# Slot attention and GELU FFN on one core: the first two batches take turns by 4, 4 and 8 chunks, with whole-chunk decoding in a new pinned order

## The chip, the cores and the metric

One core of a Trainium2 chip runs the whole program. The metric is the device time of one execution in microseconds (us), taken as the median of several runs. Lower is better.

## What is computed

Inputs are q, k, v (8 batches x 8 heads x 576 x 64), phi (8 x 8 x 576 x 32), and the weights w_in (512 x 2048) and w_out (2048 x 512).

```python
a = exp(phi - phi.max(axis=2)); a /= a.sum(axis=2) + 1e-9        # over the 576 positions
k_m = einsum('bhsm,bhsd->bhmd', a, k)                            # 32 slots per head
v_m = einsum('bhsm,bhsd->bhmd', a, v)
s = (q @ k_m.T) / sqrt(64)
p = exp(s - s.max(-1)); p /= p.sum(-1) + 1e-9
x = (p @ v_m).transpose(0, 2, 1, 3).reshape(4608, 512)           # heads side by side
h = x @ w_in
out = (0.5 * h * (1 + erf(h / sqrt(2)))) @ w_out
```

The result is float32. The weights arrive as float64 and are handed over as pairs of 32-bit words.

## The kernel before

**Algebra.** x is never formed. For each batch, v_m is multiplied into w_in first, which gives U (256 slots x 2048), and the hidden layer is p times U. Every float32 factor of the large products is split into a high part (fp32r) and a low part, and each product is three matmuls: high by high, high by low, low by high.

**Steps.** The 2048 columns of d_ff are 16 chunks f of 128. A step is one chunk of one batch: `hidden` (L671) runs 12 matmuls of 288 columns (two halves `hf` of the 576 rows) into the PSUM tag h; `gelu` (L685) on ScalarE writes gf; `gelu_hi` (L693) copies gf to gh, and `gelu_lo` (L696) on VectorE subtracts gh from gf to make gl; `project` (L714) runs 12 matmuls of 512 columns (L710) into four PSUM accumulators, acc0 to acc3. The products of a step are issued behind the hidden matmuls of the next one. The last 64 rows of each batch are collected in `tails` and projected for two batches at a time.

**Turns.** The batches come one after the other, 16 steps each, but the first two alternate: chunks 0 to 7 of batch 0, 0 to 7 of batch 1, 8 to 15 of batch 0, 8 to 15 of batch 1 (L657). One accumulator set serves one turn. At the end of a turn `evict` (L736) empties it: at the end of the first turn of a batch by a copy to an SBUF tile `part` (accumulators 0 and 2 by VectorE, 1 and 3 by ScalarE), at the end of the last turn by adding `part` and the accumulator into the output tile (L748, on VectorE).

**Decoding.** While batches 0 and 1 run, each chunk of the weights is turned from float64 words to float32, 512 columns of w_in and 512 of w_out: `dec_b` on ScalarE (L202, L203), `dec_c` on VectorE (L207, L208), `dec_s` on VectorE (L214), `dec_d` on GpSimd (L224, one add for each half), and for w_out the split into wo_hi on ScalarE (`dec_e`) and wo_lo on VectorE (`dec_f`, L230). In `dec_b`, `dec_c` and `dec_s` a second argument picks one half (128x512); without it both are done at once (128x1024).

**U and the scores.** `u_p` (L628) makes pu, a product of v_m with decoded w_in, for 1, 2 or 4 chunks; `u_h` and `u_l` (L634, L639) split it into U, on ScalarE and VectorE. `UPS` (L804) says how many chunks one such piece takes for batch 0; batch 1 always takes 4. The scores of batch 1 (psc, then `sT`, `max`, `sub`, `exp`, `sum`, `inv`, `mul`, `pT`, `ph`, `pl`) go on beside the first steps. pu, the scores psc and the slot sums pk share one PSUM buffer pair, so each of them waits until the one ahead of it has been read out.

**Order.** `START` (L22) is a list of pieces that pins the order of every engine's instructions from the program's begin into step 20 or so: names with batch, half or chunk, as `dB.3.0` for the first half of `dec_b` of chunk 3, `p.0.2` for the products of batch 0, chunk 2, and `gh.0.3:a` for a piece placed on ScalarE. Behind it, `put` gives each piece a due time in half steps, and the loop at L882 issues what is due. `prepare` (L807) puts there what a later batch needs for its softmax over phi: loads, maxima, the exponentials `aexp` with their sums, and `anat` (`a_nat`, L357), which adds the negated maxima to phi in its natural layout and takes the exponential again, for 512 rows and then for the last 64. Between `gelu` and an exponential ScalarE loads another function table.

## Time and profile before

| | us |
|---|---|
| median of 3 runs (lowest, highest) | 735.03 (734.57, 737.3) |
| profiled execution, own time | 736.67 |
| its span in the profile | 734.9 |

| engine | busy us | share of the span |
|---|---|---|
| TensorE (PE) | 712.2 | 97% |
| VectorE (DVE) | 395.5 | 54% |
| ScalarE (ACT) | 349.5 | 48% |
| GpSimd (POOL) | 47.9 | 7% |

The mean granted TensorE clock was 0.997 of its full level. Start times below count from the span's start. Between two instructions of one engine the starts are closer together than the busy times, since neighbours overlap a little: where the text speaks of what an instruction costs its engine, it is the distance from its start to the next one's.

### The profile page before, as it was taken

The numbers are of one execution on the slowest core, as the hardware profiler recorded it, in microseconds if no ns is written. First come the engines' busy times: TensorE is split into PE (matmuls) and PEld (weight loads), VectorE is DVE, ScalarE is ACT, GpSimd is POOL, SyncE is SP. The second block draws the span as 40 slices with busy tenths as digits, with TensorE's granted clock in tenths as the row PEclk, the third lists the DMA queues.
The fourth block names the chain that finished last, engine by engine and source line by source line (L and its number), as shares of the span: only waits on it lengthen the run. The fifth ranks groups of instructions, "written<-read, shape, count | busy, mean of one in ns | idle before, by whom it ended". The sixth has DMA issues, their size and how long they took to land.

```text
span 734.9 us, 12195 instructions
## 1 busy us (share of the span) xinstructions
PE 712.2 (97%) x4958; PEld 580.6 (79%) x4958; DVE 395.5 (54%) x686; ACT 349.5 (48%) x715; POOL 47.9 (7%) x45
## 2 busy tenths in 40 slices
...
GB/s 292 349 207 120 50 220 100 131 1 185 137 105 90 106 135 95 1 237 62 33 1 58 193 63 33 1 204 15 47 1 58 47 33 0 1 58 1 1 1 71
DMA packets 42584, 65.15 MB, mean 89 GB/s; under 512 B 2848, under 2 KB 24992, under 8 KB 42528
## 3 DMA queue, kind: packets, MB, share of 16 engines
...
q14 instruction: 17, 0.14, 0.1%
...
## 4 chain that ended last, share of the span: by engine, by line
PE 87%; DVE 4%; ACT 3%; issue 3%; DMA 2%; SPq 0%; POOL 0%; ACTq 0%; DVEq 0%; POOLq 0%
PE acc L710 45%; PE h L678 26%; PE tacc L710 6%; PE pu L439 4%; DMA kv<-kv 2%; PE psc L381 1%; PE psc L439 1%; PE psc L456 1%; DVE raw L208 1%; PE pk L381 1%; DVE gl L697 1%; DVE y L207 1%; ACT L688 0%; ACT L298 0%; DVE o L748 0%
## 5 line engine op out<-in xcount | busy, mean ns | idle before, releaser
L678 PE MATMUL h<-p_hi,U 128*128 128x288 f32 x1024 | 207.2, 301 | 2.6 <-ACT tails L691 1.3
L710 PE MATMUL acc<-wo_hi,gh 128*128 128x512 f32 x512 | 202.9, 397 | 0.0
L710 PE MATMUL acc<-wo_hi,gl 128*128 128x512 f32 x512 | 201.6, 394 | 0.0
L710 PE MATMUL acc<-wo_lo,gh 128*128 128x512 f32 x512 | 201.3, 393 | 0.0
L678 PEld LDWEIGHTS h<-p_hi,U 128*128 128x128 f32 x1024 | 165.2, 190 | 24.4 <-issue 6.3
L155 DVE CAST gh<-gf 128x512 fp32r<-128x512 f32 x108 | 46.0, 426 | 209.5 <-ACT gf L690 209.3
L688 ACT ACTIVATE gf<-h 128x288 f32<-128x288 f32 x128 | 52.8, 412 | 220.2 <-issue 160.2
L710 PEld LDWEIGHTS acc<-wo_hi,gh 128*128 128x128 f32 x512 | 96.1, 188 | 33.9 <-DVE gh L155 6.7
L710 PEld LDWEIGHTS acc<-wo_hi,gl 128*128 128x128 f32 x512 | 96.1, 188 | 22.7 <-DVE gh L155 0.8
L678 PE MATMUL h<-p_lo,U 128*128 128x288 f32 x512 | 110.6, 298 | 0.4 <-DVE p_lo L534 0.4
L710 PEld LDWEIGHTS acc<-wo_lo,gh 128*128 128x128 f32 x512 | 96.1, 188 | 17.4 <-issue 0.4
L697 DVE TENSOR_TENSOR gl<-gf,gh 128x512 fp32r<-128x512 f32 x128 | 89.9, 702 | 10.2 <-ACT gh L155 2.1
L678 PEld LDWEIGHTS h<-p_lo,U 128*128 128x128 f32 x512 | 83.8, 190 | 2.0 <-DVE p_lo L534 1.0
L690 ACT ACTIVATE gf<-h 128x224 f32<-128x224 f32 x128 | 45.6, 356 | 40.5 <-PE h L678 40.3
L688 ACT ACT_TABLE_LOAD x30 | 38.5, 1283 | 19.0 <-PE h L678 17.3
L641 DVE TENSOR_TENSOR U<-pu,U 128x1024 fp32r<-128x1024 f32 (+2 forms) x39 | 40.0, 1025 | 12.6 <-ACT U L155 12.3
L155 ACT CAST U<-pu 128x1024 fp32r<-128x1024 f32 (+2 forms) x39 | 33.8, 867 | 20.2 <-PE pu L439 20.1
L439 PE MATMUL pu<-w_in_sb,kT 64*32 64x512 f32 (+2 forms) x624 | 38.0, 531 | 2.5 <-DVE U L641 2.1
L208 DVE SCALAR_TENSOR_TENSOR raw<-raw 128x512 int32<-128x512 int32 (+1 forms) x33 | 36.6, 1108 | 0.3
L691 ACT ACTIVATE tails<-h 128x64 f32<-128x64 f32 x128 | 28.3, 221 | 0.0
L224 POOL TENSOR_TENSOR w_in_sb<-y,raw 128x512 int32<-128x512 int32 x16 | 23.0, 1440 | 54.8 <-DVE y L214 51.0
L202 ACT ACTIVATE y<-raw 128x512 f32<-128x512 f32 (+1 forms) x33 | 22.9, 695 | 7.7 <-DVE wo_lo L230 3.7
...
## 6 DMA issues: line engine op xcount, KB each, us to landing
...
```

The source lines that it names most:

```text
L155: return e.copy(dst, src) if e is nc.scalar else e.tensor_copy(dst, src)
L202: nc.scalar.activation(y, high.bitcast(F32), AF.Abs, scale=2.0**16)
L208: nc.vector.scalar_tensor_tensor(low, high, -(2**31), low, op0=ALU.bitwise_and, op1=ALU.bitwise_or)
L224: nc.gpsimd.tensor_tensor(w, y, low, op=ALU.add)
L439: nc.tensor.matmul(ps[g][M * j : M * j + M], st["kT", b][rows, t, M * j : M * j + M], moving[rows, j, :], start=True, stop=True,)
L641: nc.vector.tensor_sub(u[:, :, 1], st["pu", b, f], u[:, :, 0].bitcast(F32))
L678: i = nc.tensor.matmul(h[:, :HS], u[g][w], x[:, g, :], start=(n == 0), stop=(n == 3 * G - 1))
L688: nc.scalar.activation(gf[:, :HS], h[:, :HS], AF.Gelu)
L690: nc.scalar.activation(gf[:, HS:], h[:, : MAIN - HS], AF.Gelu)
L691: nc.scalar.activation(tails()[:, f, b % 2], h[:, MAIN - HS : HS], AF.Gelu)
L697: nc.vector.tensor_tensor(g_of("gl", b, f), g_of("gf", b, f), g_of("gh", b, f).bitcast(F32), op=ALU.subtract)
L710: nc.tensor.matmul(acc, x, w[:, f, :], start=(first and n == 0), stop=(last and n == 2))
```

## The change

- The first two batches take turns by chunks 0 to 3, 4 to 7 and 8 to 15, so there are six turns where there were four. The middle turn finds a `part` there already, and `evict` adds its accumulators to it, all four on VectorE.
- `a_nat` does both additions first (the 64 rows ahead of the 512) and then both exponentials; `prepare` puts `aexp` and `anorm` beside `anat`, at `tn + 1` in place of `t + 3`.
- U of batch 0 is made for single chunks 0 to 3 and then for pairs 4 and 6 (singles 0 to 7 before).
- `START` is written anew. Chunk 0 alone is decoded in halves, the others whole, with instructions of 1024 columns; k and v of batch 0, and part of q, are loaded ahead of the first weights. Chunk 15, which before was decoded by halves in START and then once more in whole by the due times (33 `dec_b` pairs in all), is decoded once (17 pairs in all).

```diff
 START = """
-Lphi.0.0 Lphi.0.1 Lwi.0 amax.0.0 Lwo.0 amax.0.1 aexp.0.0 aexp.0.1 Lkv0.0.0 at.0.0.0
...
+Lphi.0.0 Lphi.0.1 Lkv0.0.0 amax.0.0 Lkv0.1.0 amax.0.1 aexp.0.0 aexp.0.1 Lq.0.0 at.0.0.0
+anorm.0 at.0.1.0 atc.0.0.0 at.0.0.4 Lwi.0 atc.0.1.0 at.0.1.4 atc.0.0.4 atc.0.1.4
...
     def a_nat(b):
 
         aT, pn, full = st["aT", b], st["pn", b], S // P
-        for x, r, n in ((aT[:, :full], 0, full), (aT[P - TL :, full:], P - TL, 1)):
+        xs = ((aT[P - TL :, full:], P - TL, 1), (aT[:, :full], 0, full))
+        for x, r, n in xs:
             nc.vector.tensor_tensor(
                 x, x, pn[r:].unsqueeze(1).to_broadcast([P - r, n, G, P]), op=ALU.add
             )
+        for x, _, _ in xs:
             nc.scalar.activation(x, x, AF.Exp)
...
     steps = []
-    for b, lo, hi in [(b, lo, lo + NF // 2) for lo in (0, NF // 2) for b in range(2)] + [
-        (b, 0, NF) for b in range(2, B)
-    ]:
+    turns = [(b, lo, hi) for lo, hi in ((0, 4), (4, 8), (8, NF)) for b in range(2)]
+    for b, lo, hi in turns + [(b, 0, NF) for b in range(2, B)]:
         steps += [(b, f, f == lo, f == hi - 1) for f in range(lo, hi)]
...
         a = st["acc", b, f][j]
+        if f < NF - 1 and ("part", b, j) in st:
+            nc.vector.tensor_add(st["part", b, j], a, st["part", b, j])
+            return
         if f < NF - 1:
...
-    UPS = {f: 1 for f in range(NF // 2)} | {8: 4, 12: 2, 14: 2}
+    UPS = {f: 1 for f in range(4)} | {4: 2, 6: 2, 8: 4, 12: 2, 14: 2}
...
-        put(t + 3, *(f"aexp.{b}.{g}" for g in range(G)), f"anorm.{b}", f"dg.{b}")
+        put(t + 3, f"dg.{b}")
         put(tn - 1, f"Lphin.{b}")
-        put(tn + 1, f"anat.{b}")
+
+        put(tn + 1, f"anat.{b}", *(f"aexp.{b}.{g}" for g in range(G)), f"anorm.{b}")
```

The whole program's instructions by engine, before and now: TensorE rows 2667 and 2665, VectorE 665 and 624, ScalarE 697 and 658 (function table loads 70 and 68), GpSimd 51 and 51, SyncE 170 and 169. These count rows of the engines' program, in which repeated instructions can share a row.

**Place 1: ScalarE, around the first p_hi copies** (`n_hi`: L530 before, L526 now; s_2 is the last part of batch 0's scores, U_0 the first U). Before:

```order
L487 ACTIVATE s_1_250<-s_1_250 128x512
L202 ACTIVATE y_317<-raw_256 128x512
L203 ACTIVATE raw_256<-raw_256 128x512
L155 COPY kT_204<-tn_202 128x128
L202 ACTIVATE y_317<-raw_256 128x512
L203 ACTIVATE raw_256<-raw_256 128x512
L155 CAST U_0_342<-pu_0_333 128x2x128
L487 ACTIVATE s_2_349<-s_2_349 128x256
L530 CAST p_hi_0_372<-pT_0_311 128x288
```

Now:

```order
L483 ACTIVATE s_2_355<-s_2_355 128x256
L149 COPY aT_330<-pt_4_357 64x128 x2
L149 CAST U_0_378<-pu_0_369 128x2x128
L196 ACTIVATE y_390<-raw_338 128x1024
L197 ACTIVATE raw_338<-raw_338 128x1024
L526 CAST p_hi_0_419<-pT_0_300 128x288
L526 CAST p_hi_0_419<-pT_1_302 128x288
L526 CAST p_hi_1_430<-pT_0_300 128x224
L526 CAST p_hi_1_430<-pT_1_302 128x224
L526 CAST p_hi_1_430<-pT_2_425 128x64 x2
```

The decoding of chunk 2 (raw_256 before, raw_338 now) stood ahead of the last exponential and of the U copy, in halves; now it stands whole, directly ahead of the p_hi copies.

**Place 2: VectorE, up to the gl of batch 0, chunk 3** (gl_3). Before:

```order
L697 TENSOR_TENSOR gl_2_651<-gf_2_601,gh_2_637 128x512
L641 TENSOR_TENSOR U_0_342<-pu_3_641,U_0_342 128x2x128
L207 TENSOR_SCALAR y_654<-y_654 128x512
L208 SCALAR_TENSOR_TENSOR raw_545<-raw_545 128x512
L547 STREAM_TRANSPOSE sT_0_682<-psc_0_663 128x288
L230 TENSOR_TENSOR wo_lo<-y_561,wo_hi 128x512
L547 STREAM_TRANSPOSE sT_0_682<-psc_0_663 128x288
L214 TENSOR_SCALAR y_654<-y_654 128x512
L558 TENSOR_REDUCE mx_0_713<-sT_0_682 128x18
L207 TENSOR_SCALAR y_654<-y_654 128x512
L208 SCALAR_TENSOR_TENSOR raw_545<-raw_545 128x512
L565 TENSOR_TENSOR sT_0_682<-sT_0_682,mx_0_713 128x576
```

Now:

```order
L692 TENSOR_TENSOR gl_2_693<-gf_2_622,gh_2_675 128x512
L224 TENSOR_TENSOR wo_lo<-y_545,wo_hi 128x512
L208 TENSOR_SCALAR y_651<-y_651 128x1024
L569 TENSOR_REDUCE smx_1_729<-sT_1_657 128x18
L575 TENSOR_SCALAR smx_1_729<-smx_1_729 128x18
L576 RECIPROCAL smx_1_729<-smx_1_729 128x18
L581 TENSOR_TENSOR sT_1_657<-sT_1_657,smx_1_729 128x576
L587 STREAM_TRANSPOSE pT_1_739<-sT_1_657 128x576
L637 TENSOR_TENSOR U_0_705<-pu_0_696,U_0_705 128x2x512
L605 TENSOR_TENSOR p_lo_1_748<-pT_1_739,p_hi_1_741 128x576
L692 TENSOR_TENSOR gl_3_762<-gf_3_715,gh_3_746 128x512
```

Before, the first half of batch 1's scores (sT_0) was begun here; now its second half (sT_1) is finished here and the U of batch 1's first four chunks is made, since batch 1 begins behind chunk 3.

**Place 3: VectorE at the end of the turn of batch 0's chunks 4 to 7, now** (gl_4 belongs to batch 1, chunk 4; the part tiles are batch 0's):

```order
L692 TENSOR_TENSOR gl_7_1142<-gf_7_1112,gh_7_1139 128x512
L201 TENSOR_SCALAR y_1145<-y_1145 128x1024
L202 SCALAR_TENSOR_TENSOR raw_1099<-raw_1099 128x1024
L224 TENSOR_TENSOR wo_lo<-y_1060,wo_hi 128x512
L692 TENSOR_TENSOR gl_4_1188<-gf_4_1163,gh_4_1185 128x512
L735 TENSOR_TENSOR part_0_823<-acc_4_0_1038,part_0_823 128x512
L735 TENSOR_TENSOR part_1_827<-acc_4_1_1039,part_1_827 128x512
L735 TENSOR_TENSOR part_2_825<-acc_4_2_1040,part_2_825 128x512
L735 TENSOR_TENSOR part_3_830<-acc_4_3_1041,part_3_830 128x512
```

The four additions stand directly behind a gl, in one piece; before there was no turn end at this place.

## Rows read from the trace of the kernel before

**Rows 1.** Windows: us, PE, PEld, DVE, ACT, POOL busy (count), PEclk, DMA share, GB/s.
```profile
0.00:20.00 20.00, 13.97 (x128) 11.95 (x128) 5.89 (x16) 9.21 (x19) 3.53 (x9) 1.00 0.94 294
20.00:40.00 20.00, 16.91 (x163) 13.12 (x163) 16.89 (x42) 11.85 (x27) 2.64 (x2) 1.00 1.00 334
40.00:60.00 20.00, 16.52 (x187) 11.97 (x187) 19.64 (x30) 14.00 (x32) 8.66 (x6) 0.95 0.52 179
60.00:80.00 20.00, 17.93 (x159) 13.51 (x158) 18.69 (x34) 15.85 (x31) 5.72 (x4) 0.96 0.25 83
...
59.00:61.00 2.00, 2.00 (x14) 1.98 (x9) 1.86 (x5) 0.50 (x2) 0.03 (x1) 0.50 0.37 48
```

**Rows 2.** Waits of PE: total us, times, longest.
```profile
PE pu L439 <- DVE U L641: 2.1, 2, 1.1
PE psc L439 <- DVE U L641: 1.8, 1, 1.8
```

**Rows 3.** Timeline of PE before 90 us: start, us, engine, line, operation.
```profile
66.17 0.45 PE L439 MATMUL pu<-w_in_sb,kT 64*32 64x128 f32 x16 [1.08 <-DVE U L641]
...
84.86 0.54 PE L678 MATMUL h<-p_hi,U 128*128 128x288 f32 x2 [1.12 <-ACT U L155]
...
88.05 0.40 PE L710 MATMUL acc<-wo_hi,gh 128*128 128x512 f32 x1
```

**Rows 4.** Chain of waits, one full step: start, us, what.
```profile
96.93 2.77 PE acc L710 x12
99.70 1.59 PE h L678 x12
```

**Rows 5.** Timeline of PE, a U product of four chunks.
```profile
122.64 1.09 PE L439 MATMUL pu<-w_in_sb,kT 64*32 64x512 f32 x16
```

**Rows 6.** Timeline of DVE, two stretches.
```profile
39.03 0.34 DVE L534 TENSOR_TENSOR p_lo<-pT,p_hi 128x64 fp32r<-128x64 f32 x2
...
43.15 0.69 DVE L208 SCALAR_TENSOR_TENSOR raw<-raw 128x512 int32<-128x512 int32 x1
43.77 0.67 DVE L697 TENSOR_TENSOR gl<-gf,gh 128x512 fp32r<-128x512 f32 x1
44.36 0.74 DVE L214 TENSOR_SCALAR y<-y 128x512 int32<-128x512 int32 x2
...
46.48 1.80 DVE L208 SCALAR_TENSOR_TENSOR raw<-raw 128x512 int32<-128x512 int32 x1
...
89.80 1.21 DVE L641 TENSOR_TENSOR U<-pu,U 128x1024 fp32r<-128x1024 f32 x1
90.93 0.67 DVE L697 TENSOR_TENSOR gl<-gf,gh 128x512 fp32r<-128x512 f32 x1
```

**Rows 7.** Timeline of POOL beside them.
```profile
46.24 1.49 POOL L224 TENSOR_TENSOR w_in_sb<-y,raw 128x512 int32<-128x512 int32 x1
```

**Rows 8.** Groups of DVE by form, 0 to 160 us: busy us, mean ns, idle before.
```profile
L208 DVE SCALAR_TENSOR_TENSOR raw<-raw 128x512 int32<-128x512 int32 x32 | 35.3, 1104 | 0.3
...
L208 DVE SCALAR_TENSOR_TENSOR raw<-raw 128x1024 int32<-128x1024 int32 x1 | 1.2, 1218 | 0.0
...
L207 DVE TENSOR_SCALAR y<-y 128x1024 f32<-128x1024 f32 x1 | 0.7, 682 | 0.0
```

**Rows 9.** ACT: a group by form of 0 to 160 us, and its timeline near 33.
```profile
L202 ACT ACTIVATE y<-raw 128x1024 f32<-128x1024 f32 x1 | 1.1, 1132 | 0.0
32.94 1.20 ACT L530 CAST p_hi<-pT 128x288 fp32r<-128x288 f32 x4 [0.21 <-PE pT L515]
```

**Rows 10.** Timeline of ACT, an exponential between two gelus.
```profile
152.24 1.28 ACT L298 ACT_TABLE_LOAD   x1
153.53 0.78 ACT L298 ACTIVATE phi<-phi,nm 128x576 f32<-128x576 f32 x1
```

**Rows 11.** Timeline of PE and DVE, 167 to 171 us.
```profile
167.40 0.54 PE L678 MATMUL h<-p_hi,U 128*128 128x288 f32 x2 [1.00 <-ACT tails L691]
...
170.55 1.88 DVE L748 TENSOR_TENSOR o<-acc,part 128x512 f32<-128x512 f32 x3
```

83 lines of the change are left out of this document (38 added, 45 removed).

## The prediction

> **What bounds the kernel now.** I read the windows first, then TensorE's waits, its timeline up to 100 us, the chain of waits, and last VectorE's and GpSimd's rows of the same stretch. TensorE is busy 712.2 of 734.9 us, so 22.7 us is all that a new order can win unless TensorE's own work changes. The windows show where that idle time lies: 6.0 us in the first 20, 3.1, 3.5 and 2.1 in the next three windows of 20 [rows 1]. From the product at 88.05 on, TensorE's groups follow each other at 2.77 us (12 products) and 1.59 us (12 hidden matmuls), 4.36 us a step [rows 3, 4], and the largest wait behind that is one of 1.0 us at 167 [rows 11]. So the gain, if any, is made before 88 us. There the window rows show VectorE busy for 19.64 and 18.69 of 20 us [rows 1], and TensorE's waits name it: for the U subtraction at L641, because pu and psc share one buffer pair [rows 2, 3]. From about 39 us to 91 us the kernel goes at VectorE's pace. Up to 40 us it goes at the pace of the transfers: the DMA share is 0.94 and 1.00, at 294 and 334 GB/s [rows 1].
>
> **Term 1, the start.** The change loads k, v and q of batch 0 ahead of the weights. On ScalarE the whole decoding of chunk 2 now stands directly ahead of the p_hi copies (the first place shown), so these wait for that chunk's transfer. In SyncE's new order the bytes up to the w_out rows of chunk 2 are, from the shapes, 0.59 (phi 0) + 2.36 (k, v 0) + 1.18 (q 0) + 2.10 (chunks 0, 1) + 0.59 (phi 1) + 2.10 (eight pieces of k, v 1) + 1.05 (chunk 2) = 9.97 MB. At the rates of before, 5.88 MB pass by 20 us and the other 4.1 MB need 12.2 us: 32.2, and I allow 1 us for landing: 33.2. The two ScalarE instructions of 1024 columns, 1.13 each [rows 9], end at 35.5. VectorE's L208 on the result, 1.14 (1.22 busy less the overlap of 0.08 that neighbours show) [rows 8], ends at 36.6, and the p_lo subtractions behind it (288, 224 and 64 columns, two each, about 1.6 by the width of the 512-wide rows) at 38.2. Meanwhile the p_hi copies, 1.20 for four and about 0.3 for the short pair [rows 9], have ended at 37.0 and are covered. Before, the last p_lo ended at 39.3 [rows 6]. **Gain 1.1 us.** The bounds: with landing in 0 us 2.1, with landing 2 us later nothing or a loss of 1.
>
> **Term 2, eight steps at VectorE's pace.** Take VectorE from the last p_lo to the gl of the eighth step (batch 0, chunk 7 before; batch 1, chunk 3 now). Costs are distances between starts [rows 6]: L208 of 512 columns 0.62, a gl 0.59, L214 0.335 (two in 0.67; L207 of the same width like it), U of four chunks 1.13; whole-chunk L207 and L214 0.60 (0.68 busy less the overlap) [rows 8]. By the order, what differs in the stretch is this:
> - L208: 12 halves, 7.4, become 6 whole, 6.8: 0.6 less; I count 0.4, since the overlap of a whole one is known from a single row.
> - L207 and L214: 24 halves, 8.0, become 12 whole, 7.2: 0.8 less.
> - U: two of four chunks and six single ones, 2.26 + 6 x 0.335 = 4.3, become one of four, two pairs (0.60, as any 512 wide) and three single ones, 3.3: 0.9 less.
> - Two copies to `part` at the first turn's end, 0.6 each: 1.2 more. The other two are ScalarE's.
>
> Eight gl, seven wo_lo and the two score sets of batch 1 stand on both sides. Together 0.9 us less. But VectorE does not go at these costs: all 81 instructions of the stretch make 39.5 us by them, and it took from 39.3 to the end of the gl at 90.93, 91.5 [rows 6], that is 52.2, or 1.32 times as long. The surplus is what GpSimd's adds cost it: an L208 took 0.69 where none ran and 1.80 beside the add at 46.24 [rows 6, 7], and the mean of 32 is 1.10 [rows 8]. The adds are 12 on both sides. So 0.9 x 1.32 = **1.25 us gained**: the eighth gl ends at 38.2 + 38.55 x 1.32 = 89.1, where before it was 91.5.
>
> **Term 3, TensorE's own work.** Four single U products of 0.38 (66.17 to the next start, 66.55) [rows 3] become two pairs of about 0.59, between that and the 1.02 of four chunks (1.09 busy) [rows 5]: **0.35 us less**.
>
> **What I cost at nothing.** The eight additions to `part` (8 x 0.6 = 4.8 us of VectorE) lie between 88 and 150 us, where TensorE has no waits; in the same stretch whole-chunk decoding and the second decoding of chunk 15 that is gone give some of it back. Without that cover each turn's end would cost up to what its additions reach past the 1.59 us of the next hidden matmuls: 2.4 - 1.6 = 0.8. The three additions in a row at 170.55, 1.88 us, held up no matmul [rows 11]. The regrouped exponentials save table loads on ScalarE (1.28 each [rows 10]); they can win part of the 1.0 us at 167, and I set 0.5 of it against 0.5 of new waits at the hand-over from batch 0 to batch 1, whose U and scores must now be ready four steps earlier. What is late next is the same thing as before, VectorE, four steps into each turn.
>
> **Sum.** 1.1 + 1.25 + 0.35 = 2.7 us. The profiled execution took 736.67 and would come to 734.0; the median of the runs is 735.03, 1.64 lower, and the forecast is made against it: **732.3 us**. Its own range is 729.5 to 735. A measurement of this kernel can tell about 0.5% from no change, 3.7 us: under 731.4 counts as faster, over 738.7 as slower.
>
> **Rivals.**
> - *GpSimd's adds miss VectorE.* With half as many instructions on VectorE and new neighbours, the adds may fall on instructions that they do not delay. The mean L208 lost 1.10 - 0.69 = 0.41 to them [rows 6, 8]; without this for 12 adds, 4.9 us: 732.3 - 4.9 = **727.4**. For it: the next bound, TensorE, leaves room, since eight steps at 4.36 are 34.9 of the 51 us. Against: adds and L208 belong to the same chunk chain, so they come close together again. Chance 0.25.
> - *The adds hit every time.* An add of 1.49 held up one L208 by 1.80 - 0.69 = 1.11 [rows 6, 7]. If each of the 12 met a long instruction, 12 x (1.11 - 0.41) = 8.4 more: **740.7**. Whole-chunk instructions are twice as long and so easier to meet, but the mean of before says that two in three were not met in full. Chance 0.04. The Trainium skill, page "SBUF — State Buffer", section Terms, has VectorE and GpSimd lock a shared port pair for a whole instruction, so that the loser "fully blocks". By that rule this rival is what any add would do when a VectorE instruction that needs the pair comes behind it; the trace agrees at the one place shown, where the L208 ended 0.55 us after the add at 47.73, nearly its whole length.
> - *The gain is given back at the turns' ends.* There are two more of them, at up to 0.8 us each if VectorE is still late there, and at the two middle ones VectorE has two additions of 0.6 that would have been ScalarE's copies, of which I let one reach past the hidden matmuls: 2 x 0.8 + 2 x 0.6 = 2.8 us: 735.1, say **735**. For it: VectorE stays above 90% busy in these windows. Against: the row at 170.55. Chance 0.11.
> - *Slower: the first step waits for the weights.* The p_hi copies have no way round the decoding of chunk 2 on ScalarE. If the chunk lands at 38 and not at 33.2, because the eight pieces of k and v of batch 1 and phi 1 ahead of it in the queue go slower, all eight steps begin 4.8 us later, and term 1 turns from +1.1 to -3.7. TensorE then stands nearly idle from 34 on, and its clock falls, as it did in the window 59 to 61, behind the wait for psc: 0.50 granted, that is 1.2 GHz, and a product group or hidden group of 1.59 takes near twice that [rows 1, 4]. I price it at 1.6 for such a group, and 0.8 for the turn's end that is then missed: 732.3 + 4.8 + 1.6 + 0.8 = **739.5**. It decides from a landing at about 36 on; the DMA was saturated over these 40 us, which speaks for it, and the byte count, which is a sum and no guess, against it. Chance 0.14.
>
> **How the numbers follow.** Forecast 0.46, the others 0.25, 0.04, 0.11 and 0.14. The range that should hold 8 in 10 reaches from just under the second case, 726.5, to just over the slower one, 740.0; the forecast's own is 729.5 to 735. A third of the forecast's chance lies under 731.4: faster is 0.25 + 0.15 = 0.40; no difference is 0.31 + 0.11 = 0.42; slower 0.14 + 0.04 = 0.18.
>
> **What would show it.** In the profile of the changed kernel: the last short p_lo pair ends near 38.2 (term 1; 41 or later is the slower rival, with p_hi copies released by L197 late). The gl of batch 1, chunk 3, ends near 89 (term 2), and VectorE stays above 90% busy from 40 to 90; if that gl ends by 85 the adds missed, and the mean of whole-chunk L208 is near 1.2, not 1.5 to 1.8. TensorE's waits still name L641. Behind 90 us there is no wait of TensorE over 1 us, and none released by an addition to `part`; if there are, the third rival holds. The prediction is wrong if TensorE's idle time before 90 us changes by more than 5 us either way, or if TensorE's busy time changes by more than 1.

## The result, and the profile after

The changed kernel took 740.88 us (median of 6 runs, 738.57 to 743.13), the kernel before 735.21 (6 runs beside it, 734.57 to 737.3). The ratio is 1.0073 [1.0059, 1.0086]: slower by 5.4 us, where a gain of 2.7 was forecast, and outside the range. The profiled execution took 740.40 us, 3.73 more than the one of before. All ratios below are against the kernel before, run on the same chip at the same time; start times come from one profiled execution of each kernel. In the changed kernel the products stand at L705, the hidden matmuls at L673, gl at L692, the subtraction of U at L637, and the decoding at L196 (ScalarE), L202 and L208 (VectorE) and L218 (GpSimd).

The page's first part, changed kernel:

```profile
PE 711.2 (96%) x4926; PEld 580.6 (79%) x4926; DVE 390.5 (53%) x646; ACT 340.8 (46%) x677; POOL 51.5 (7%) x45
```

TensorE's work is 1.0 us less and the span 3.7 us more, so TensorE stands idle 4.7 us longer. The same windows as [rows 1]:

```profile
0.00:20.00 20.00, 13.07 (x195) 11.26 (x195) 8.60 (x18) 8.71 (x18) 3.54 (x9) 0.77 0.94 297
20.00:40.00 20.00, 16.45 (x129) 13.53 (x121) 17.01 (x37) 12.44 (x25) 2.91 (x2) 0.59 1.06 352
40.00:60.00 20.00, 15.64 (x156) 10.93 (x154) 16.13 (x25) 15.17 (x26) 8.17 (x6) 0.87 0.55 186
60.00:80.00 20.00, 17.61 (x118) 13.12 (x119) 19.52 (x28) 16.28 (x29) 4.21 (x4) 0.83 0.16 53
```

From 40 to 80 us TensorE is busy 33.25 us where it was 34.45. VectorE falls from 19.64 to 16.13 of 20 between 40 and 60, and is full, 19.52, between 60 and 80. TensorE's waits, the whole run:

```profile
PE h L673 <- ACT tails L686: 4.2, 4, 1.6
PE psc L452 <- ACT k_blocks L149: 3.1, 1, 3.1
PE pu L435 <- DVE sT L543: 1.9, 1, 1.9
PE h L673 <- DVE U L637: 1.5, 1, 1.5
```

Behind 100 us, the first of these was one wait of 1.0 before [rows 11]; it is four now, 4.2 together. TensorE's timeline (start, us, operation, and the wait ahead of it) shows three of the four, and between them the product groups by which I count the steps:

```profile
49.14 0.39 PE L705 MATMUL acc<-wo_hi,gh 128*128 128x512 f32 x1
...
71.14 0.43 PE L673 MATMUL h<-p_hi,U 128*128 128x288 f32 x2
...
93.25 0.40 PE L705 MATMUL acc<-wo_hi,gh 128*128 128x512 f32 x1
...
150.43 0.54 PE L673 MATMUL h<-p_hi,U 128*128 128x288 f32 x2 [1.37 <-ACT tails L686]
...
152.38 0.50 PE L705 MATMUL acc<-wo_hi,gl 128*128 128x512 f32 x1 [0.42 <-DVE gl L692]
...
170.90 0.53 PE L673 MATMUL h<-p_hi,U 128*128 128x288 f32 x2 [1.64 <-ACT tails L686]
...
371.95 0.54 PE L673 MATMUL h<-p_hi,U 128*128 128x288 f32 x2 [0.58 <-ACT tails L686]
```

The start of the first product matmul of a step, by TensorE's timeline of each kernel (E5, E13 and E17 are experiments below), in us:

| step | before | changed | E5 | E13 | E17 |
|---|---|---|---|---|---|
| first | 44.55 | 49.14 | 46.35 | 49.54 | 48.13 |
| fifth | 73.40 | 77.89 | 75.53 | 74.89 | 73.54 |
| eighth | 92.41 | 93.25 | 91.18 | 88.75 | 87.40 |
| 14th | 119.78 | 120.91 | 118.84 | 117.86 | 116.54 |
| 19th | 143.56 | 144.68 | 142.61 | 147.69 | 142.93 |
| 24th | 168.30 | 171.79 | 167.26 | 176.17 | 169.96 |
| end of the span | 734.9 | 738.6 | 734.3 | 743.3 | 737.7 |

Two losses can be read off. The changed kernel is 4.6 us late at the first product, makes 3.7 of it good by the eighth, and keeps 1.1 up to the 19th. Then it loses another 2.4 between the 19th and the 24th: 27.11 us, where before it was 24.74. Behind that the two go alike, to 0.2 us. The first loss is the less firm of the two: E5 has the changed kernel's order up to the eighth product, and there its profile is 1.2 us ahead of the kernel before.

**The second loss, 146 to 171 us, stands in ScalarE's timeline:**

```profile
146.41 0.62 ACT L149 CAST wo_hi<-y 128x512 fp32r<-128x512 f32 x1 [5.42 <-POOL y L218]
146.94 0.41 ACT L683 ACTIVATE gf<-h 128x288 f32<-128x288 f32 x1
...
149.39 0.62 ACT L149 CAST wo_hi<-y 128x512 fp32r<-128x512 f32 x1 [2.04 <-POOL y L218]
149.91 0.35 ACT L685 ACTIVATE gf<-h 128x224 f32<-128x224 f32 x1
...
168.00 1.06 ACT L360 ACTIVATE aT<-aT 128x1024 f32<-128x1024 f32 x1
169.08 1.28 ACT L685 ACT_TABLE_LOAD   x1
170.37 0.36 ACT L685 ACTIVATE gf<-h 128x224 f32<-128x224 f32 x1
```

The copies to wo_hi of chunks 14 and 15 stand ahead of gelus in ScalarE's order and wait for GpSimd's add, 5.42 and 2.04 us; the gelus wait behind them, and TensorE behind the gelus (1.37 at 150.43, 0.42 at 152.38). The adds were late because VectorE's L208 of these chunks was: GpSimd had stood 11.15 us for it (its line is in the last section). START ends at chunk 15's `dec_c`; what is left of chunks 14 and 15 goes out by the due times, which know nothing of that. And the regrouped exponentials put the long one, 1.06 us of 1024 columns, between two halves of a gelu, with its table load: 1.64 us at 170.90 where there was 1.00 [rows 11].

**The first loss.** VectorE's timeline:

```profile
37.90 0.65 DVE L530 TENSOR_TENSOR p_lo<-pT,p_hi 128x224 fp32r<-128x224 f32 x3
...
42.39 0.35 DVE L391 TENSOR_SCALAR km<-pk,rz 128x128 f32<-128x128 f32 x1 [2.38 <-PE pk L377]
...
49.71 2.33 DVE L202 SCALAR_TENSOR_TENSOR raw<-raw 128x1024 int32<-128x1024 int32 x1
...
60.70 1.22 DVE L202 SCALAR_TENSOR_TENSOR raw<-raw 128x1024 int32<-128x1024 int32 x1
...
71.80 0.68 DVE L692 TENSOR_TENSOR gl<-gf,gh 128x512 fp32r<-128x512 f32 x1
...
81.04 1.79 DVE L692 TENSOR_TENSOR gl<-gf,gh 128x512 fp32r<-128x512 f32 x1
...
89.87 0.68 DVE L692 TENSOR_TENSOR gl<-gf,gh 128x512 fp32r<-128x512 f32 x1
```

The last p_lo ended at 38.55 (forecast 38.2) and the eighth gl at 90.55 (forecast 89.1; 91.5 before). So VectorE did come through sooner than before, by 1.0 us, and the kernel was late all the same: the eighth product starts 2.7 us behind that gl, where before it started 0.9 us behind. The fourth gl, the last of batch 0's first turn, comes only at 71.80. From the hidden matmul at 71.14 to the eighth product TensorE has no wait that the profile lists: it needs 22.1 us for four steps and three U products. Only at the first matmul of the sixth step that reads gl it is late, by about 0.2 us, because the sixth gl (the row at 81.04) ended at 82.83. TensorE's timeline:

```profile
82.48 0.40 PE L705 MATMUL acc<-wo_lo,gh 128*128 128x512 f32 x1
82.89 0.50 PE L705 MATMUL acc<-wo_hi,gl 128*128 128x512 f32 x1
```

So less work for VectorE behind 71 us would hardly have ended these steps sooner, but up to the sixth gl VectorE had no room for more either (E15).

Ahead of 71 us TensorE's waits for the transposes and for U (1.9, 0.5 and 1.5 us between 58 and 63.6) stand next to a low granted clock, about the level of 1.2 GHz. Window of the changed kernel:

```profile
62.00:69.00 7.00, 5.48 (x28) 3.23 (x28) 6.90 (x11) 4.33 (x7) 2.55 (x2) 0.51 0.00 0
```

The U product of four chunks at 64.41 took 1.96 us there, the one at 91.33, at a clock of 1.00, 1.09. No run takes this low stretch away, so its share of the loss is not known.

### The profile page after: what moved, and what is told of

Same layout as the page of the kernel before. It is cut to its first block, busy times and chain, and to the rows that moved or that the text cites. A ratio compares the mean times of both kernels' runs of the same rounds, so it can differ in the third digit from the quotient of the medians.

```text
span 738.6 us, 12063 instructions
## 1 busy us (share of the span) xinstructions
PE 711.2 (96%) x4926; PEld 580.6 (79%) x4926; DVE 390.5 (53%) x646; ACT 340.8 (46%) x677; POOL 51.5 (7%) x45
## 4 chain that ended last, share of the span: by engine, by line
PE 77%; issue 1%; DVE 1%; ACT 1%; POOL 0%; ACTq 0%; DVEq 0%
PE acc L705 41%; PE h L673 23%; PE tacc L705 6%; PE pu L435 3%; PE psc L377 1%; PE psc L435 1%; PE pk L377 1%; PE tn L349 0%; POOL y L218 0%; DVE aT L356 0%; DVE gl L692 0%; POOL w_in_sb L218 0%; PE tn L401 0%; ACT gf L685 0%; ACT L685 0%
## 5 line engine op out<-in xcount | busy, mean ns | idle before, releaser
L673 PE MATMUL h<-p_hi,U 128*128 128x288 f32 x1024 | 208.1, 301 | 7.2 <-ACT tails L686 4.2
L705 PE MATMUL acc<-wo_hi,gh 128*128 128x512 f32 x512 | 203.0, 396 | 0.0
L705 PE MATMUL acc<-wo_hi,gl 128*128 128x512 f32 x512 | 201.4, 394 | 0.5 <-DVE gl L692 0.4
L705 PE MATMUL acc<-wo_lo,gh 128*128 128x512 f32 x512 | 201.5, 394 | 0.0
L673 PEld LDWEIGHTS h<-p_hi,U 128*128 128x128 f32 x1024 | 165.9, 190 | 30.9 <-issue 8.9
L705 PEld LDWEIGHTS acc<-wo_hi,gh 128*128 128x128 f32 x512 | 96.4, 188 | 33.1 <-DVE gh L149 7.5
L705 PEld LDWEIGHTS acc<-wo_hi,gl 128*128 128x128 f32 x512 | 96.0, 188 | 24.0 <-DVE gl L692 1.8
L673 PE MATMUL h<-p_lo,U 128*128 128x288 f32 x512 | 110.5, 297 | 0.5 <-DVE p_lo L530 0.5
L705 PEld LDWEIGHTS acc<-wo_lo,gh 128*128 128x128 f32 x512 | 96.2, 188 | 17.4 <-issue 0.4
L692 DVE TENSOR_TENSOR gl<-gf,gh 128x512 fp32r<-128x512 f32 x128 | 93.0, 727 | 11.8 <-ACT gh L149 3.2
L673 PEld LDWEIGHTS h<-p_lo,U 128*128 128x128 f32 x512 | 83.9, 190 | 1.5 <-DVE p_lo L530 0.8
L637 DVE TENSOR_TENSOR U<-pu,U 128x1024 fp32r<-128x1024 f32 (+2 forms) x37 | 39.7, 1073 | 15.4 <-ACT U L149 15.4
L218 POOL TENSOR_TENSOR w_in_sb<-y,raw 128x512 int32<-128x512 int32 x16 | 24.0, 1498 | 97.7 <-DVE y L208 90.6
L543 DVE STREAM_TRANSPOSE sT<-psc 128x288 f32<-128x288 f32 x28 | 12.0, 463 | 30.5 <-PE psc L377 24.5
L218 POOL TENSOR_TENSOR y<-y,raw 128x512 int32<-128x512 int32 x16 | 25.5, 1596 | 1.3 <-DVE y L208 1.3
```

The costliest lines, as they stand in the source:

```text
L218: nc.gpsimd.tensor_tensor(w, y, low, op=ALU.add)
L543: nc.vector.transpose(sT[:, g].rearrange("p a m -> p (a m)"), st["ps", b, hf, g][:, :HS])
L637: nc.vector.tensor_sub(u[:, :, 1], st["pu", b, f], u[:, :, 0].bitcast(F32))
L673: i = nc.tensor.matmul(h[:, :HS], u[g][w], x[:, g, :], start=(n == 0), stop=(n == 3 * G - 1))
L692: nc.vector.tensor_tensor(g_of("gl", b, f), g_of("gf", b, f), g_of("gh", b, f).bitcast(F32), op=ALU.subtract)
L705: nc.tensor.matmul(acc, x, w[:, f, :], start=(first and n == 0), stop=(last and n == 2))
```

## The experiments

E1 to E6 and E8 to E17 are edits of the changed kernel, E7 of the kernel before. TensorE's wait lines of several of them stand together below E5.

**E1: the exponentials as before, nothing else undone.**

```diff
-        xs = ((aT[P - TL :, full:], P - TL, 1), (aT[:, :full], 0, full))
-        for x, r, n in xs:
+        for x, r, n in ((aT[:, :full], 0, full), (aT[P - TL :, full:], P - TL, 1)):
...
-        put(t + 3, f"dg.{b}")
+        put(t + 3, *(f"aexp.{b}.{g}" for g in range(G)), f"anorm.{b}", f"dg.{b}")
```

> The changed kernel with a_nat and prepare as they were before (512 rows first, each exponential right behind its addition, aexp at t + 3). Theory 1, that the regrouped exponentials hold up gelu: TensorE's wait of 1.64 us at 170.9 goes back to the 1.00 of before, and the two waits of 0.58 at 372 and 463 vanish: 1.8 us faster than the changed kernel, 739.1 against 740.9. Rival, that these waits come from the new turns and only fall at another place: no difference beyond 0.5 us. No gain at all beyond 90 us would also fall to the view that all of the loss lies in the first 90 us.

Measured: 741.84, ratio 1.0071 [1.0053, 1.0089], no gain. The waits of 0.58 at 371.95 and 463.01 went and the 1.64 became 1.0, but the exponentials, at their old due time again, now stood ahead of gelus together with the late copy of chunk 15, and TensorE lost 1.6 us between the 20th and 21st step. From the 19th step to the 24th it took 28.03.

**E2: the rest of chunks 14 and 15 pinned behind gelus.** START goes on behind its old last piece:

```diff
-dC.15
+dC.15 gelu.0.10.1 dS.14 gh.0.10 dDi.14 dS.15 gl.0.10 p.0.9 dDo.14 h.0.11.0 gelu.0.11.0
+h.0.11.1 dDi.15 gelu.0.11.1 dE.14 p.0.10 gh.0.11 gl.0.11 dDo.15 dF.14 h.0.12.0 Up.0.14.2
...
```

> The changed kernel with its pinned order carried on for two and a half steps, so that ScalarE copies wo_hi of chunks 14 and 15 behind the gelus of steps 11 and 12 and not ahead of them. Theory 2, that ScalarE, waiting 5.42 and 2.04 us for GpSimd's adds, held up those gelus: TensorE's waits of 1.37 at 150.4 and 0.42 at 152.4 vanish: 1.8 us faster, 739.1. Rival, that the wait is only moved, to the next function table load or to the U of chunks 14 and 15: TensorE waits for another name between 146 and 160 us by about as much, and the time stays.

Measured: 738.30, ratio 1.0027 [1.0017, 1.0036]. The waits of 1.37 and 0.42 are gone, the stage from the 19th step to the 24th takes 25.28 us, 1.8 less, and the median is 2.6 us lower. Of the pieces that were tried this is the largest. The edit also pins VectorE's and GpSimd's last work on both chunks, so it does not tell late copies from late adds.

**E5: E1 and E2 together.**

> The changed kernel with both edits of the two runs before: a_nat and prepare as before, and the pinned order carried on so that wo_hi of chunks 14 and 15 is copied behind the gelus. Each alone left a wait of TensorE near 150 us. Theory: the two share ScalarE's queue there, so that only both together give the stage back: from the product of step 18 to that of step 23 it takes 24.7 us, as before the change (27.1 in the changed kernel), and the waits of 0.58 at 372 and 463 are gone: 2.4 + 1.2 = 3.6 us faster than the changed kernel, 1.2 to 2.2 us slower than the kernel before. Rival, that the new turns cost there: over 26 us from step 18 to 23.

Measured: 738.05, ratio 1.0023 [1.001, 1.0036]; from the 19th step to the 24th 24.65 us, as before. TensorE's waits for the tails, 140 to 500 us, in E1, E2 and E5:

```profile
PE h L671 <- ACT tails L684: 2.4, 2, 1.4
```
```profile
PE h L673 <- ACT tails L686: 2.8, 3, 1.6
```
```profile
PE h L671 <- ACT tails L684: 1.0, 1, 1.0
```

E5 leaves the single wait of 1.0 that the kernel before has. So the second loss is explained by these two edits in its place. E5 against E2 shows no difference in the median: the waits of the regrouping, though seen, are not worth what they add up to.

**E7: the regrouped exponentials alone, in the kernel before.** The edit is E1's, the other way round.

> The kernel before with that part of the change alone which regroups the exponentials: a_nat's order, and aexp and anorm beside anat. Theory 1: the wait of 1.00 us at 167 becomes 1.64, and two waits of 0.58 come in, at the scores' exponentials of later batches: 1.8 us slower than the kernel before. Rival, that those waits need the new turns or the late chunks 14 and 15: within 0.5 us of the kernel before. If the regrouping does what it is written for, fewer table loads, it is faster by up to the 1.0 us of that wait.

Measured: 735.84, ratio 1.0 [0.9988, 1.0012]. The same three waits come in:

```profile
PE h L680 <- ACT tails L693: 2.8, 3, 1.6
```

That is 1.8 us more than before, and the time is the same. What gives it back was not found.

**E3 and E4: two reasons for the late first product.** E3 moves the first chunk's `dec_b` and `dec_c` behind batch 0's transposed k:

```diff
-slots.0.0.0 Lwo.0 slots.0.1.0 km.0.0.0 Lkv0.0.1 dB.0.0 km.0.1.0 slotsT.0.0 Lkv0.1.1
-dC.0.0 kT.0.0 dB.0.1 n_score.0 dS.0.0 Lq.0.1 dC.0.1 dDi.0 dS.0.1 Lwi.1 slots.0.0.1
+slots.0.0.0 Lwo.0 slots.0.1.0 km.0.0.0 Lkv0.0.1 km.0.1.0 slotsT.0.0 Lkv0.1.1
+kT.0.0 dB.0.0 dC.0.0 dB.0.1 n_score.0 dS.0.0 Lq.0.1 dC.0.1 dDi.0 dS.0.1 Lwi.1 slots.0.0.1
```

> The changed kernel with one piece moved on ScalarE: the copy to k_blocks ahead of dec_b of chunk 0, which waits until 12.4 us for its transfer. TensorE then need not stand still from 11.0 to 14.1. Theory 3, that this gap drops TensorE's clock to 1.2 GHz, and the low clock makes the first steps late: the granted clock stays at 1.0 well past 12 us, the first hidden matmuls of chunk 0 take 1.6 us and not 2.9, the product of batch 0, chunk 0, starts 1.5 to 3 us before 49.1, and the time falls by 1.5 to 3. Rival, that the first steps wait for transfers and for ScalarE's and VectorE's queues whatever the clock: the product starts within 0.5 us of 49.1 and the time stays within 1 us.

Measured: 739.89, ratio 1.0053 [1.0036, 1.007]; first product 49.18. The granted clock fell all the same, to 0.55 from 10 to 20 us, so the run says nothing on theory 3. E4 puts the decoding of chunk 2 behind the p_hi copies, which is the undoing of what I feared most:

```diff
-Lwi.3 atc.1.0.4 atc.1.1.4 n_mul.1 Up.0.0.1 dDi.1 n_sum.2 n_T.1 Uh.0.0 Lwo.3 n_inv.2 dB.2
-Ul.0.0 n_mul.2 slots.1.0 dDo.1 Lq.1.0 n_hi.0 dC.2 n_T.2 Lkv.1.1.3 n_hi.1 Lkv.1.1.4
-n_hi.2 Lwi.4 dE.1 n_lo.0 n_lo.1 h.0.0.0 Lwo.4 n_lo.2 gelu.0.0.0 km.1.0 h.0.0.1 dF.1
+Lwi.3 atc.1.0.4 atc.1.1.4 n_mul.1 Up.0.0.1 dDi.1 n_sum.2 n_T.1 Uh.0.0 Lwo.3 n_inv.2
+Ul.0.0 n_mul.2 slots.1.0 dDo.1 Lq.1.0 n_hi.0 n_T.2 Lkv.1.1.3 n_hi.1 Lkv.1.1.4
+n_hi.2 dB.2 Lwi.4 dE.1 n_lo.0 n_lo.1 h.0.0.0 Lwo.4 n_lo.2 dC.2 gelu.0.0.0 km.1.0 h.0.0.1 dF.1
```

> The changed kernel with the decoding of chunk 2 behind the p_hi copies on ScalarE and behind the p_lo subtractions on VectorE. The predicted slower rival, that the first step waits for the weights: p_hi starts near 32 in place of 35.6, the first hidden matmuls near 35 in place of 37.4, and the product of chunk 0 comes 1 to 2 us earlier; the time falls by as much if TensorE keeps that lead. Rival, that the low clock and the queue behind the first gelu set the pace: under 0.5 us, or slower, because chunk 2 is then ready later for its own step.

Measured: 741.32, ratio 1.0075 [1.0051, 1.0099]. The copies no longer wait for the weights, ScalarE's timeline of E4:

```profile
32.65 1.20 ACT L526 CAST p_hi<-pT 128x288 fp32r<-128x288 f32 x4 [0.34 <-PE pT L511]
```

and the first product comes at 50.03 all the same (the granted clock from 40 to 50 us was 0.66 here, 0.75 in the changed kernel). The three microseconds won at p_hi are lost again before the first product: the weights are not what it waits for.

**E6 and E8: TensorE's clock.** In the windows above the granted clock is 0.77, 0.59, 0.87 and 0.83, where before it was 1.00, 1.00, 0.95 and 0.96 [rows 1]. E6 adds 29 matmuls of ones by ones between 9 and 32 us, whose result nobody reads:

```diff
-slots.0.0.0 Lwo.0 slots.0.1.0 km.0.0.0 Lkv0.0.1 dB.0.0 km.0.1.0 slotsT.0.0 Lkv0.1.1
+slots.0.0.0 warm.3.1 Lwo.0 slots.0.1.0 km.0.0.0 Lkv0.0.1 dB.0.0 km.0.1.0 slotsT.0.0 warm.14.1 Lkv0.1.1
...
+    def warm(n, early):
...
+        for _ in range(n):
+            nc.tensor.matmul(t[:, :P], ones, ones, start=True, stop=True)
```

> The changed kernel with 29 extra matmuls of 128x128 on constants, whose results nobody reads, put into TensorE's gaps up to 33 us (2, 3 and 14 of them before 14 us; 4, 3 and 3 between 28 and 33). Theory 3, that TensorE's low clock up to 42 us makes the first steps late: the granted clock stays at 1.0 past 11 us, the hidden matmuls of chunk 0 and the slot sums of batch 1 take 1.6 and 1.4 us in place of 2.9 and 2.1, the product of batch 0, chunk 0, starts near 47 in place of 49.1, and the time falls by 1.5 to 2.5 us. Rival, that transfers and the queues of ScalarE and VectorE set the first steps: clock at 1.0, but the product within 0.7 us of where it was and no change in the time. If the clock falls at 11 us all the same, the run tells nothing on either.

Measured: 740.76, ratio 1.0062 [1.0047, 1.0077]; first product 49.38. The granted clock was 1.00 from 10 to 20 us and 0.57 from 20 to 30, so what a clock held up through 42 us would give stays open:

```profile
10.00:20.00 10.00, 7.83 (x164) 6.84 (x152) 5.28 (x11) 3.85 (x8) 2.59 (x2) 1.00 1.09 343
20.00:30.00 10.00, 7.38 (x38) 6.77 (x39) 8.35 (x18) 5.81 (x12) 0.00 (x0) 0.57 1.06 354
```

E8 is E5 with these matmuls:

> The changed kernel with all three edits: exponentials as before, the pinned order carried on, and the extra matmuls. If the loss of 5.4 us is the sum of these three places and nothing is left for the new turns themselves, it comes out within 1 us of the kernel before. If it is the turns and their additions that cost, it stays 2 us or more slower. If the predicted gain of the shorter first turn is there once the clock holds, it is 1 to 3 us faster.

Measured: 739.24, ratio 1.0044 [1.0027, 1.0061], not better than E5. Its granted clock was 0.83 and 0.88 in the two windows of 10 us from 20 to 40, and 0.67 from 40 to 50; its first product came at 49.22. What the clock of this stretch is worth is shown by chance in E7, which is the kernel before up to here. Windows of E7, and its first product:

```profile
10.00:20.00 10.00, 7.45 (x100) 6.42 (x101) 2.28 (x7) 3.76 (x9) 2.57 (x2) 0.50 1.09 342
20.00:40.00 20.00, 16.76 (x164) 13.09 (x165) 16.97 (x41) 11.56 (x27) 2.63 (x2) 0.53 0.99 329
```
```profile
44.82 0.50 PE L712 MATMUL acc<-wo_hi,gh 128*128 128x512 f32 x1
```

At 0.50, the level of 1.2 GHz, almost through from 10 to 40 us, the first product came at 44.82; in the profile of before, at 1.00, at 44.55. While the transfers set the pace, half the clock cost 0.3 us, by one profile of each. Later a low clock and a late first product go together: in profiles with the changed kernel's order up to here, the first product comes at 46.35 with a granted clock of 1.00 from 40 to 50 us (E5), at 49.14 with 0.75 (changed kernel), at 50.37 with 0.67 (E1) and at 50.41 with 0.50 (E2). Which of the two makes the other is not shown. From the first product to the eighth all four take 44.1 to 45.0 us, so the first loss differs from run to run ahead of the first product.

**E9 and E10: batch 0's first steps ahead of batch 1's slot sums and scores.**

```diff
-slots.1.1 dS.2 gelu.0.0.1 dDi.2 dB.3 km.1.1 slotsT.1 dDo.2 kT.1 dC.3 gh.0.0:a Up.0.1.1
...
+Up.0.1.1 dS.2 gelu.0.0.1 Uh.0.1 Ul.0.1 dDi.2 gh.0.0:a gl.0.0 dB.3 h.0.1.0 h.0.1.1 dDo.2
+Lwi.5 slots.1.1 gelu.0.1.0 Lwo.5 gelu.0.1.1 p.0.0 km.1.1 slotsT.1 dE.2 kT.1 dC.3 dF.2 Lq.1.1
...
```

> The changed kernel with one stretch of its order turned round: U and the hidden matmuls of batch 0, chunk 1, and with them the first product, ahead of the slot sums, the transposes and the first scores of batch 1. Theory 4, that the shorter first turn puts batch 1's preparation ahead of batch 0's first product, where the one PSUM pair makes a chain (slot sums, km, transposes, kT, U, scores), and that TensorE stands still on this chain: the product of chunk 0 starts at 43 to 45 in place of 49.1, TensorE's idle time from 40 to 64 falls by 2 us or more, and the products from the fifth step on come 1.5 to 3 us earlier; the time falls by as much. Rival, that VectorE's sum of work sets the eighth step whatever the order: the first product comes earlier, but the eighth within 0.7 us of where it was, and the time stays. A second rival, that the scores of batch 1 are then too late: a new wait of TensorE before the fifth step, and a slower kernel.

Measured: 740.62, ratio 1.0061 [1.004, 1.0082]. The first product came at 46.49, but batch 1's km, which was at 42.39, came behind it, so the scores came later too, and the eighth product at 95.29. That is no gain; nor is it a sure loss, for E1, whose first steps are the changed kernel's, has 95.41 there. VectorE's timeline of E9:

```profile
46.63 0.35 DVE L391 TENSOR_SCALAR km<-pk,rz 128x128 f32<-128x128 f32 x1 [3.26 <-PE pk L377]
```

E10 is E9 with E5:

> The same edit together with the two at the late place (exponentials as before, pinned order carried on). By theory 4 and the late place together the changed kernel's loss is all accounted for: 735 to 736, within 1 us of the kernel before. If it comes out faster than that by 1.5 us or more, the forecast gain of the shorter first turn was there, under the two losses; if it stays at 738, the first steps' order is not what costs.

Measured: 738.97, ratio 1.0047 [1.0032, 1.0062], not better than E5.

**E11 and E12: no wait for the buffer pair.** pu of batch 0's chunks 1 to 3 goes into columns of batch 1's score tiles that are free, so U is no longer held up by the scores; in START, U of chunk 3 is moved ahead of the transposes of these scores.

```diff
-        pu = st["pu", b, f] = banks("pu", b, f)[:, :, : n * P]
+        if b == 0 and 1 <= f <= 3:
+            pu = st["pu", b, f] = banks("psc", 1, f // 3)[:, :, FB - P :]
+        else:
+            pu = st["pu", b, f] = banks("pu", b, f)[:, :, : n * P]
```

> The changed kernel, where pu of batch 0's chunks 1, 2 and 3 is written into free columns of the score tiles of batch 1 and not into a tile of its own, so that scores no longer wait for the U subtractions at L637 nor pu for the score transposes at L543; and U of chunk 3 is taken ahead of these transposes in the pinned order. Theory 4, that TensorE stands still from 40 to 64 us because batch 1's preparation and batch 0's U share one PSUM pair: the waits of 1.2 (psc for L637), 1.9 (pu for L543) and 1.5 (hidden matmuls for L637) go, the third product starts at 61 to 64 in place of 67.9, the fifth at 73 to 75.5 in place of 77.9, the eighth at 90 to 92 in place of 93.3, and the time falls by 1.5 to 3. Rival, that VectorE's sum of work is the pace: the third product comes earlier, but TensorE stands still as long further on, and the eighth product stays within 0.7 us of 93.3.

Measured: 742.62, ratio 1.0084 [1.0067, 1.01]. TensorE's timeline of E11:

```profile
62.77 0.39 PE L708 MATMUL acc<-wo_hi,gh 128*128 128x512 f32 x1
...
68.90 0.54 PE L676 MATMUL h<-p_hi,U 128*128 128x288 f32 x2 [3.22 <-ACT U L149]
...
71.54 0.85 PE L676 MATMUL h<-p_hi,U 128*128 128x288 f32 x2 [1.84 <-DVE U L640]
```

The third product came at 62.77, 5.1 us sooner than 67.91, and then TensorE stood still for batch 1's U, 3.22 and 1.84: the whole gain. The eighth product came at 95.46. E12 is E11 with E5:

> The same with the two edits at the late place (exponentials as before, pinned order carried on), which alone gave 738.05 against 736.04 for the kernel before. By theory 4 it comes to 735 to 736.5, level with the kernel before or a little faster; by the rival it stays at 738.

Measured: 739.83, ratio 1.0045 [1.003, 1.0061]. So neither the order of the first steps nor the buffer pair, changed by itself, let batch 1's first step start sooner: the fifth product came at 79.63 in E9 and 80.38 in E11, at 77.89 in the changed kernel.

**E13: decoding one chunk later.** E5, with every piece of the decoding of chunks 5 and up, its loads and its U products, moved back in START to the place of the next chunk. VectorE is so freed of one chunk's decoding ahead of batch 1's preparation, and of one ahead of the eighth gl as well: five whole chunks stand there and not six. Two lines of the rewritten 24, as an example:

```diff
-gelu.0.2.0 h.0.2.1 sum.1.0 dDi.4 p.0.1 inv.1.0 gelu.0.2.1 mul.1.0 dB.5 dDo.4 pT.1.0
-sT.1.1.0 Lwi.7 sT.1.1.1 ph.1.0 dC.5 Up.0.3.1 gh.0.2:a Lwo.7 Uh.0.3 dE.4 pl.1.0 max.1.1
+gelu.0.2.0 h.0.2.1 sum.1.0 dDi.4 p.0.1 inv.1.0 gelu.0.2.1 mul.1.0 dDo.4 pT.1.0
+sT.1.1.0 Lwi.7 sT.1.1.1 ph.1.0 Up.0.3.1 gh.0.2:a Lwo.7 Uh.0.3 dE.4 pl.1.0 max.1.1
...
```

> The changed kernel with both edits of the late place, and with the decoding of every chunk from 5 on moved back by one chunk's place in the pinned order, its loads and the U products that need it with it, so that four chunks and not five are decoded ahead of batch 1's first step. Theory 5, that VectorE's work ahead of the fourth gl sets the start of batch 1, and TensorE the pace behind it: the gl of batch 0, chunk 3, at 67 to 69 in place of 71.8, the fifth product at 72.5 to 74.5 in place of 77.9, the eighth at 88 to 90 in place of 93.3, and the time 3 to 5 us under that of the run with the late edits alone: 733 to 735, faster than the kernel before. Rival, that the pace of these steps is set by ScalarE, the PSUM pair and the transfers: the gl within 1 us of 71.8 and the time at 738. A second rival, that the decoding, a chunk later, now holds up a later step: the eighth product earlier, but new waits of TensorE between 95 and 170 us that give it back.

Measured: the fourth gl at 69.60, the eighth product at 88.75, 4.5 us sooner than in the changed kernel and 3.7 sooner than before, with the first product no sooner (49.54). Of the 4.5 us, 1.6 are TensorE's own work put off: the U products at 85.39 and 91.33 in the changed kernel (0.59 and 1.02 to the next start) stand behind the eighth product here. From the first product to the eighth E13 takes 39.2 us, against 44.1 to 45.0 in the changed order; E5, of which it is an edit, had the eighth product at 91.18 with a first product 3.2 us sooner. The whole is slower, 744.60, ratio 1.0101 [1.0067, 1.0135]: GpSimd's adds then come too late for the U products. VectorE's gl, then TensorE's timeline of E13:

```profile
69.60 0.68 DVE L690 TENSOR_TENSOR gl<-gf,gh 128x512 fp32r<-128x512 f32 x1
```
```profile
88.75 0.40 PE L703 MATMUL acc<-wo_hi,gh 128*128 128x512 f32 x1
...
122.66 0.66 PE L433 MATMUL pu<-w_in_sb,kT 64*32 64x512 f32 x8 [1.87 <-POOL w_in_sb L218]
...
159.48 0.67 PE L433 MATMUL pu<-w_in_sb,kT 64*32 64x256 f32 x16 [2.92 <-POOL w_in_sb L218]
```

**E17: E13, with U asked for later.** U of batch 0's chunks 8 to 11 stands one group later, and that of chunks 12 to 15 is made singly.

```diff
-    UPS = {f: 1 for f in range(4)} | {4: 2, 6: 2, 8: 4, 12: 2, 14: 2}
...
-h.1.6.0 Uh.0.8 dDo.11 dS.12 h.1.6.1 gelu.1.6.0 gelu.1.6.1 p.1.5 dE.11 Ul.0.8 dDi.12
...
+gh.1.6:a dF.10 dDo.11 gl.1.6 dB.12 h.1.7.0 Up.0.8.4 h.1.7.1 gelu.1.7.0 Uh.0.8 Ul.0.8 dC.12 dE.11
...
```

> The run with the decoding one chunk later, and in it the U of chunks 8 to 11 asked for one group of hidden matmuls later, and that of chunks 12 to 15 for single chunks, each right ahead of its step, so that no U product stands behind an add that is still to come. If the early gain is real and only lost at these waits (1.9 + 1.2 + 2.9 us), it comes out 5 to 6 us under that run, 738 to 740, with the eighth product again at 88 to 90. If VectorE's backlog takes it back, other waits of TensorE (for gl, U or wo_lo) come in their place and the time stays over 742.

Measured: 739.92, ratio 1.0051 [1.0034, 1.0068]. The lead over the kernel before is 5.0 us at the eighth product, part of it U products put off as in E13, and still 0.6 at the 19th, then it is lost: a new wait of 2.1 for the tails stands at batch 2's exponentials. TensorE's waits in E17, 95 to 300 us:

```profile
PE h L671 <- ACT tails L684: 2.1, 1, 2.1
PE pu L433 <- POOL w_in_sb L218: 1.1, 1, 1.1
```

**E14, E15 and E16: the same extra work for VectorE, early or late.** The clamp of a chunk (L201) is repeated, which changes nothing in its result: eight times more over chunks 3 to 5, or eight times more over chunks 6 to 8. At 0.60 each that is 4.8 us. E16 is the changed kernel again, on the same chip.

```diff
-        nc.vector.tensor_scalar(y, y, 2.0, W_MAX, op0=ALU.max, op1=ALU.min)
+        for _ in range({3: 4, 4: 4, 5: 3}.get(f, 1)):
+            nc.vector.tensor_scalar(y, y, 2.0, W_MAX, op0=ALU.max, op1=ALU.min)
```

> The changed kernel with the clamp of dec_c (L201, 128x1024, 0.60 us) done 4, 4 and 3 times for chunks 3, 4 and 5: 8 more instructions, 4.8 us of VectorE, ahead of the fourth gl; repeated, the clamp changes nothing. Theory 5: nearly all of it goes into the time: the fourth gl and the eighth product 3.5 to 5 us later, and 3.5 to 5 us slower than the changed kernel. Rival, that VectorE has slack there (it is busy for 16.1 of 20 us from 40 to 60): under 2 us.

> The same 8 clamps for chunks 6, 7 and 8 (4, 4 and 3 times), behind the fourth gl and in the four steps of batch 1. Theory 5: TensorE sets the pace there, so most of it is hidden: the eighth product less than 2 us later, the time less than 2 us slower. Rival, the prediction's own term 2, that all eight steps go at VectorE's pace: as slow as with the clamps in the first four steps, 3.5 to 5 us.

> The changed kernel itself, as the measure for the three beside it on the same chip: 740 to 742, 4.5 to 6 us slower than the kernel before.

Measured: E14 745.32, ratio 1.0124 [1.0107, 1.014]; E15 744.96, 1.011 [1.0084, 1.0135]; E16 741.34, 1.0069 [1.0052, 1.0086]. E14 is 4.0 us over E16, and its eighth product 5.0 later, at 98.27 against 93.25: there, early work on VectorE costs its full length. E15 cost nearly as much, 3.6 us, and its eighth product came at 98.64, 5.4 later: theory 5, by which most of it is hidden, failed there, and the rival came, the prediction's own term 2. TensorE waits for the sixth gl, 2.6 us that the changed kernel does not have (the other 0.4 of the line it has too). Waits of E15, and its timeline of TensorE:

```profile
PE acc L706 <- DVE gl L693: 3.0, 2, 2.6
```
```profile
86.71 0.68 PE L706 MATMUL acc<-wo_hi,gl 128*128 128x512 f32 x1 [2.56 <-DVE gl L693]
```

So VectorE has no slack up to the sixth gl, two steps into batch 1's turn. E13 takes one chunk's decoding out of the stretch ahead of the fourth gl and out of that ahead of the eighth, so it does not tell the two apart; nor does it follow that there was free room for this work later.

No kernel here was faster than the one before. Of the edits of the changed kernel the best are E2 and E5.

## Why the prediction was wrong

**Term 1, the start: right.** The last p_lo ended at 38.55 against 38.2. Chunk 2's decoding waited for its transfer and began at 33.52 against 33.2 (one of the eight pieces of k and v is half as high as the others, which makes 0.13 MB and 0.4 us less in the sum). ScalarE's timeline:

```profile
33.52 1.14 ACT L196 ACTIVATE y<-raw 128x1024 f32<-128x1024 f32 x1 [2.02 <-DMA raw<-w_out]
```

That held the copies up by 3 us, which did not matter (E4). The bounds of landing were wider than needed. But the term stopped at p_lo. Behind it TensorE's first product came at 49.14, 4.6 us later than before, and that stretch had no term.

**Term 2, eight steps at VectorE's pace: this is the step that failed.** I added up VectorE's instructions from the last p_lo to the eighth gl as one lump and took the end of the lump for the end of TensorE's eight steps. With the 0.9 us of before between that gl and the eighth product, the forecast puts the product at about 90.0; it came at 93.25. VectorE's lump is 1.5 us of this: the gl ended at 90.55 against 89.1. The same stretch, from the last p_lo to the end of the eighth gl, before and now:

```profile
39.37:91.60 52.23, 45.55 (x422) 33.78 (x423) 49.58 (x83) 40.23 (x82) 17.32 (x12) 0.97 0.35 116
```
```profile
38.55:90.55 52.00, 45.23 (x347) 33.78 (x346) 47.63 (x64) 38.62 (x68) 18.22 (x12) 0.87 0.41 137
```

VectorE's work did fall, by 1.95 us, but it stood idle for 4.4 us where it had been 2.7; between 40 and 60 it was 81% busy, not over 90 as I had said, and among others waited 2.38 us for the slot sums pk. (So not all of the surplus of before was the adds' either: 2.7 of it was idle time.) The other 1.8 us lie behind VectorE: the last gl that TensorE had to wait for is the sixth, at 82.83, and from there it needs 10.4 us at its own pace, two U products among them, to the eighth product. An end of the lump is not the end of the steps.

The mechanism that I offer is the due time. With turns of eight, the preparation of batch 1 (scores, p, U) was due only behind the eighth step, and TensorE had eight steps to do in the meantime. With turns of four it is due behind the fourth, and VectorE has ahead of it the decoding of chunks that nobody needs until the ninth step. The prediction named this hand-over and priced it at 0.5. Shown is that VectorE's work sets the pace up to the fourth gl (E14) and on to the sixth (E15), and that one chunk's decoding less in this stretch makes it 3 to 4 us shorter (E13, without the U products put off). E9 and E11 show that what is won ahead of batch 1's preparation, at the first product or the third, is given back at its U. That the earlier due time is what cost is argued from the order: no run changes it alone. The granted clock is a rival for part of it: in E5, with 1.00 from 40 to 50 us, the eighth product came 1.2 us sooner than before, half of the gain that was forecast for it.

**Term 3: right.** TensorE's busy time fell by 1.0 us; the 0.35 of the U products are part of it, and records can be missing.

**The late places, costed at nothing: failed, by 2.4 us.** For the exponentials I had even set down a gain of 0.5. I looked at VectorE's additions and at the exponentials there, and not at what the due times do with the rest of chunks 14 and 15. The new place of two wo_hi copies in ScalarE's order, behind GpSimd's adds and ahead of gelus, was to be seen in the order; their waits were 5.42 and 2.04 us. E2 removes these waits and 1.8 of the 2.4 us, E5 all of them.

**The rivals.** That the adds miss VectorE did not come: L202 of a whole chunk took 1.22 us clear of adds and 2.33 beside one, with a mean of 1.52 over 15. That they hit every time did not come either, for the same mean. The Trainium skill, page "SBUF — State Buffer", section Terms, has the loser of the shared port pair wait out the other's instruction; the 2.33 agrees, and the 1.22 at 60.70 shows that not every one meets an add. The additions at the turns' ends (L735) released no wait of TensorE in the changed kernel's profile, so that rival did not come. The slower rival named 739.5 us, near what came, and for a wrong reason: E4 took its cause away and gained nothing. A forecast that misses a mechanism is not saved by a rival with the right number.

**The sum.** By the profiles the loss is 3.7 us: about 1.1 up to the 19th step, 2.4 from there to the 24th, 0.2 behind. The medians differ by 2 us more. The changed kernel's eighth product came at 93.25 in E16 and in its own profile, while edits far behind it, which ought not to move it, gave 95.41 (E1), 94.51 (E2) and 91.18 (E5); and E5's median, with the second loss gone, is still 2.0 over the kernel before, although its profile, of one of its quickest runs, has a span of only 734.3. With the late place mended, the medians of E2 and E5 are 2.2 and 2.0 us over the kernel before; from these I estimate the first loss at about 2 us in most runs. What makes it differ between runs is open.
